# Apply step of the second LayerNorm on GpSimd for three chunks, tail out-projection in one piece, planner constants set anew

## The chip, the cores and the metric

The kernel runs on one core of a Trainium2 chip. Its time is the device time of one execution in microseconds, and the median of several executions is what counts. The core has five engines that each work through their own instruction list in order: TensorE (PE in the profile, its weight loads PEld), VectorE (DVE), ScalarE (ACT), GpSimd (POOL) and SyncE (SP), which here only issues DMAs. Instructions of different engines are ordered by semaphores alone.

## The reference, cut to what matters

The input `x` has 2048 tokens of 640 features. A small product of `c` gives six modulation vectors; then attention with 32 heads of 20 features and a gated bilinear block follow, each behind a LayerNorm without weights.

```python
mod = (silu(c) @ w_mod).reshape(1, 6, 1, 640)
sa, ca, ga, sb, cb, gb = (mod[:, i] for i in range(6))
h = layernorm(x) * (1 + ca) + sa          # first LayerNorm
q, k, v = split(h @ wqkv)                 # 32 heads of 20
p = softmax(q @ k.T * 20 ** -0.5)         # 2048 x 2048 for each head
x = x + ga * ((p @ v) @ wo)               # out-projection
h = layernorm(x) * (1 + cb) + sb          # second LayerNorm
x = x + gb * (((h @ w_gate) * (h @ w_up)) @ w_down)
```

`layernorm(x)` is `(x - mean) / sqrt(var + 1e-5)`. The last step of it, the apply step, takes mean and reciprocal deviation as given and computes `(x - mean) * rs` for each token.

## The kernel before, in words

**Stages.** The queries are cut into five chunks (`CHUNKS`, L431): three of 512 tokens (0 to 2) and two of 256 (3 and 4). Heads are taken four at a time, so a chunk has eight items, 40 in all. For an item PE computes scores against all 2048 keys (L1403), in PSUM banks; a score block is then exponentiated and PE multiplies it with V into bank 7 (L1957). An item ends with a transpose on DVE (L1587), a reciprocal of the softmax sums (L1590), a multiplication on POOL (L1592), a second DVE transpose into `OcT` (L1599) and DMAs on SP's queue that put the rows in place in `Ocp` (L1611).

**Two ways to the exponential.** Most score blocks go to ACT: one Exp over two banks (128x1024), from group 580 on (`HEADG`) over two and three banks in turn (L1439). The others, 99 quads of four blocks (`QUADS` says how many for each item), go to DVE, which builds the exponential from integer operations: an evacuation of each block (L1463), two bit operations (L1495, L1503) and a product (L1500). A block on DVE costs PE two products with V, not one.

**The suffix of a chunk** (function `suffix`) is what follows attention: the out-projection in rounds of 320 columns (L866, in the last chunk L862), its residual sum on DVE (L1682), the second LayerNorm by tiles of 128 tokens, the transposes (L1715) with their evacuation into `h2T` (L1720), the gate and up products with `hprod` (L1815, L1784), and the down product with its residual sum (L1838) and the store. The suffix of chunk 0 runs beside the attention of chunk 1, and so on. Only that of chunk 4, the tail, has no attention beside it. What is left of chunk 3's suffix when attention ends is done there too.

**The second LayerNorm of a tile** is: two statistics instructions (L1696), their aggregation (L1698), epsilon added on POOL (L1699; in the tail on DVE), the power -0.5 on POOL (L1701), and the apply step on DVE (L1703) into `xn2`. The transposes of a chunk outside the tail wait for all of its tiles: four for chunks 0 to 2, two for chunks 3 and 4. The profile leaves digits off names, so `xn2` of chunks 0 to 2 reads `xn`, `mv2` reads `mv`, `rs2` reads `rs`.

**The tail's out-projection.** With `OP_EARLY = 1` each of its four rounds is in two pieces: five matmuls on `Ocp` (rows of the items that are done) may go ahead, and a sixth on `OcT` of the last item is a task of its own that waits for the second transpose (L1599).

**What sets the order.** The kernel's Python holds a planner (class `Sched`): each instruction is a `Task` with an engine, an estimated duration, dependencies and a priority, and a simulated clock picks for each engine the ready task of least priority number. The order found is written out as five fixed instruction lists with semaphore waits. Constants shape it: `GATE_F` spreads the rounds of a chunk's suffix over the next chunk's Exp groups; `HT_L`, `V_L`, `K_LEAD`, `KD_LEAD`, `LATE_A` and `LATE_L` say how far ahead of their item projections are due; `D_LEAD` and `D_RES` place the DVE blocks; `PVMIN`, `PVMAX` and `PVCAP` size batches of products with V; `STEAL_GAP` limits when ACT takes over evacuations from DVE, which it may do in the first 66 us of the plan. Tasks marked `lk` use what DVE and POOL share: the planner never lets one of DVE and one of POOL with that mark overlap. With `lk` 2 a POOL task also yields to any ready DVE task with the mark, and gets a dependency on the last such DVE task.

Of the kernel before, what the change touches and what calls it, by code (L numbers as in the profile page):

```python
# [6 lines left out]
ALU = mybir.AluOpType  # L7
# [18 lines left out]
DMA_SLOW = 0.0015  # L26
DMA_LAT = 1700.0
STEAL_END = 66197.894
STEAL_GAP = 184.697
HAM_W = 3413.3  # L30
HAM_MIN = 2550.0

# [288 lines left out]
def emit_program(nc, sched, nsem_dma=56):  # L321
# [83 lines left out]
    with nc.Block() as block:  # L405
# [20 lines left out]
        def _(e):  # L426
# [4 lines left out]
CHUNKS = ((0, 512), (512, 512), (1024, 512), (1536, 256), (1792, 256))  # L431
QUADS = ((0, 4, 3, 3, 4, 3, 4, 3),
# [4 lines left out]
D_LEAD = 0.383  # L437
NB0, NSS = 2, 3
HEADG = 580
OP_EARLY = 1  # L440
EV_OP = 0.5
T_SPLIT = 1
GU_OUTER = 4
# [1 line left out]
LN2T = 0.6  # L445
# [4 lines left out]
XBACK = 1  # L450
HOLD = 110
PVTOL = 253
XDPRIO = 2.163
TPRIO = 0.75
TAHEAD = 1
GU_ONE = 1
# [3 lines left out]
NPS = 4  # L460
TS_4X, TT_2X = 600.0, 1145.0
WM_GATE = 9
WM_NEED = 1.814
K_DIRECT = (0, 1, 2, 3)
Q_DIRECT = 2
K_LEAD = 0.705
K_ALL = (0,)
KD_LEAD = 0.216
DMA_WINDOW = 900000
D_LATE = 16  # L470
D_RES = 58
PVMIN, PVMAX, PVCAP = 4, 14, 13
PV0 = 0
V_PARTS = [[0, 4], [4, 8]]
V_L1 = 0.2
# [7 lines left out]
PREEMPT = 0.0  # L483
PRE_M = 0.3
PV0N = 1
GATE_F = (0.925, 0.688, 1.105, 0.744, 1.0)
FILL_MIN = 4156.882
FILL_HARD = 0.0
FILL_T0, FILL_TH, FILL_MINH = 2300.0, 17000.0, 7500.0
# [3 lines left out]
LN_POOL = ()  # L493
LN_ACT = [1, 3, 5, 7]
XFIRST = 0
LN2P = 2.447
NALT = 1
OPFIRST = 0
HT_L = 0.105
V_L = 0.225  # L500
LATE_A = 4.5
LATE_L = 2.493
LATEQ = (3,)
LATEQ_A = 2
LATEQ_F = 0.581
QUAD_GAIN = 0.597233983857778
NTERM = 2
XHALF = 1
# [12 lines left out]
def build_kernel(nc, A_x, A_wqkv, A_wo, B_x, B_w_gate, B_w_up, B_w_down, c, w_mod, out):  # L521
# [60 lines left out]
    mhalf = alloc("mhalf", [128, 4], F32)  # L582
# [14 lines left out]
    mv2 = alloc("mv2", [128, NT, 2], F32)  # L597
    sd2 = alloc("sd2", [128, NT], F32)
    rs2 = alloc("rs2", [128, NT], F32)
    invT = alloc("invT", [128, 16], F32)  # L600
# [24 lines left out]
    OT = alloc("OT", [128, 512], F32)  # L625
# [27 lines left out]
    xck = R2.alloc("xck", [128, 4, D], BF16)  # L653
    xn2 = R2.alloc("xn2", [128, 4, D], BF16)
# [57 lines left out]
    def dve(dur, f, deps=(), prio=3.0, **k):  # L712
        return sc.add(Task("dve", dur, f, deps, prio=prio, **k))
# [6 lines left out]
    def pool(dur, f, deps=(), prio=3.0, **k):  # L720
        t = Task("pool", dur, f, deps, prio=prio, **k)
        t.lk = 1
        return sc.add(t)

    def dvl(dur, f, deps=(), prio=3.0, **k):
        t = Task("dve", dur, f, deps, prio=prio, **k)
        t.lk = 1
        return sc.add(t)
# [58 lines left out]
    def load_rest():  # L787
# [5 lines left out]
        for q, f in enumerate((first2[0], first2[1],  # L793
# [12 lines left out]
    p_i0 = pool(150, lambda e: e.memset(ident[:], 0.0), prio=0)  # L806
    p_id = pool(300, lambda e: e.affine_select(ident[:], ident[:], pattern=[[-1, 128]], compare_op=ALU.not_equal,
                                               fill=1.0, base=0, channel_multiplier=1), [p_i0], prio=0)
    p_mh = pool(100, lambda e: e.memset(mhalf[:], -0.5), prio=1)
    p_on = dve(600, lambda e: e.memset(Vf[:, :].rearrange("p (h w) -> p h w", w=VW)[:, :, 0:1], 1.0), prio=-1)  # L810
    d_pz = dve(500, lambda e: e.memset(ps[:, BPV, :], 0.0), [], prio=3.5)
    d_wz = [dve(70, lambda e, w=w: e.memset(w[:, :, D:WKQ], 0.0), prio=0) for w in (wk_sb, wq_sb)]
# [413 lines left out]
    items = [(ci, j) for ci in range(NC) for j in range(NSET)]  # L1226
# [10 lines left out]
    for it, (ci, j) in enumerate(items):  # L1237
        q0, n = CHUNKS[ci]
# [231 lines left out]
    for qi, (it, us) in enumerate(dquads):  # L1470
# [36 lines left out]
        if X_POOL and qi % X_POOL == X_POOL - 1 and qi < len(dquads) - X_LAST and all(  # L1507
# [22 lines left out]
            t = term(fx, [tm, te], TT_2X, "X", src=0, last=True)  # L1530
# [48 lines left out]
    def item_end_tasks(it):  # L1579
        ci, j = items[it]  # L1580
        if ci == NC - 1 and j == 0:
            z_tail[ci] = [pool(1200, lambda e: e.memset(Ocp[:, ci % 2, KD - 1, :], 0.0), list(oc_free[ci - 2]), prio=9)]
        n = CHUNKS[ci][1]
        nb32 = n // 32
        slot = ci % 2
        cell = {}
        t1 = Task("dve", n * 1.1 + 70, lambda e: e.transpose(OT[:, 0:n], ps[:, BPV, 0:n]), [], prio=0.0, name=f"T1.{it}")  # L1587
        t1.acq = [(sOT, "o", 1)]
        item_info[it]["t1"] = t1
        t2 = dve(155, lambda e: e.reciprocal(invT[:, 0:nb32].unsqueeze(2),  # L1590
                                            OT[:, 0:n].rearrange("p (b c) -> p b c", c=32)[:, :, 0:1]), [t1], prio=1.5)
        f3 = lambda e: e.tensor_tensor(  # L1592
            OTn[:, 0:n].rearrange("p (b c) -> p b c", c=32), OT[:, 0:n].rearrange("p (b c) -> p b c", c=32),
            invT[:, 0:nb32].unsqueeze(2).to_broadcast([128, nb32, 32]), ALU.mult)
        if T3_POOL and it < len(items) - 1:
            t3 = pool(n * 2.2 + 200, f3, [t2], prio=0)
        else:
            t3 = dvl(sb_cost(n, 1.04), f3, [t2], prio=1.5)
        t4 = dve(n * 1.1 + 65, lambda e: e.transpose(OcT[:, cell["s"], 0:n], OTn[:, 0:n]), [t3], prio=1.5)  # L1599
        direct = j == NSET - 1 and ci == NC - 1  # L1600
        pcs = [] if direct else oc_pieces(j)
        t4.acq = [(sOcT, "s", max(1, len(pcs)))]

        def on4(task):
            cell["s"] = task.slots["s"]
            sOT.done(0, task)
# [27 lines left out]
    def suffix(ci):  # L1634
# [28 lines left out]
        t_xn2 = []  # L1663
        x1_done = []
        op_last = []
        for tl in range(ntl):
            ev = []
            for hf in range(2):
                mms = []
                for k in range(KD):  # L1670
                    f = qf(320, lambda k=k, tl=tl: Ocp[:, slot, k, tl * 128:(tl + 1) * 128],
                                 lambda k=k, hf=hf: wo_sb[:, k, 320 * hf:320 * hf + 320], k == 0, k == KD - 1 and not tail)
                    mms.append((C320, f))
                fx = qf(320, lambda tl=tl: OcT[:, oc_last[ci]["s"], tl * 128:(tl + 1) * 128],
                              lambda hf=hf: wo7[:, 320 * hf:320 * hf + 320], False, True)
                if tail and not OP_EARLY:
                    mms.append((C320, fx))

                pq = pr(True)

                def after(r, tl=tl, hf=hf, fx=fx, pq=pq):
                    f = lambda e: e.tensor_tensor(xck[:, tl, 320 * hf:320 * hf + 320], ps[:, r.b["b"], 0:320],  # L1682
                                                  xck[:, tl, 320 * hf:320 * hf + 320], ALU.add)
                    if tail and OP_EARLY:
                        fs_ = fx if isinstance(fx, list) else [fx]
                        r.last = sc.add(Task("pe", C320, [lambda e, g_=g_: g_(e, r.b["b"]) for g_ in fs_], [r.last, oc_ready[ci][-1]],
                                             ctr="pex", prio=pq - 1000, name=f"op{ci}.{tl}", mode=r.last.mode))
                    return [dve(ps_cost(320), f, [r.last, d_xc], prio=EV_OP if tail else 1)]
                r = Round(mms, list(oc_ready[ci][:-1] if tail and OP_EARLY else oc_ready[ci]) + t_wo + [d_xc], after, pq, gate=gate(KD * 320),
                          name=f"op{ci}.{tl}")  # L1690
                ev.append(r.evac[0])
                op_last.append(r.last)
            t = t0 + tl
            bn = []
            for hf in range(2):
                bn.append(dve(ps_cost(320), lambda e, tl=tl, hf=hf: e.bn_stats(  # L1696
                    st2[:, tl, 6 * hf:6 * hf + 6], xck[:, tl, 320 * hf:320 * hf + 320]), [ev[hf]], prio=LN2T if tail else LN2P))
            ag = dve(115, lambda e, t=t, tl=tl: e.bn_aggr(mv2[:, t, :], st2[:, tl, :]), bn, prio=LN2T if tail else LN2P)  # L1698
            f1 = lambda e, t=t: e.tensor_scalar(sd2[:, t:t + 1], mv2[:, t, 1:2], EPS, None, op0=ALU.add)  # L1699
            p1 = dve(75, f1, [ag], prio=LN2T if tail else LN2P) if tail else pool(220, f1, [ag], prio=1)  # L1700
            p2 = pool(570, lambda e, t=t: e.tensor_tensor(rs2[:, t:t + 1], sd2[:, t:t + 1], mhalf[:, 0:1], ALU.pow),  # L1701
                      [p1], prio=1)
            t_xn2.append(dvl(360, lambda e, t=t, tl=tl: e.tensor_scalar(  # L1703
                xn2[:, tl, :], xck[:, tl, :], mv2[:, t, 0:1], rs2[:, t:t + 1], op0=ALU.subtract, op1=ALU.mult),
                [p2] + first, prio=LN2T if tail else LN2P))
            x1_done += ev
        oc_free[ci] = op_last[-1:]
        if tail:
# [644 lines left out]
```

## Time and profile before

| what | value |
|---|---|
| median of three executions | 817.66 us (817.46 to 822.7) |
| profiled execution, its own time | 816.77 us |
| its span, first to last instruction | 815.0 us |
| granted TensorE clock | 1.0 throughout |
| ACT busy | 775.9 us, of which Exp (777 instructions) 756.9 us |
| PE busy | 787.8 us |
| DVE busy | 722.7 us |
| POOL busy | 73.3 us |
| first Exp starts, last Exp ends | 16.30 us, 782.43 us |
| apply steps of chunks 0 to 2 on DVE | 12 instructions, 427 ns each on average |
| filler matmuls of PE (L2277), which keep its clock up | 27.3 us |

The profiled execution took 1.8 us more than its span, and the median lies 0.9 us above the profiled execution. "Busy" is the time in which an engine had an instruction in work; instructions of one engine overlap a little, so the mean of one times the count is more than the busy time. Idle time of an engine is put down to the engine whose semaphore came last.

### The profile page before, as it was taken

To read this page: it belongs to the slowest core of one execution; us is meant where nothing else is said; L and a number is where in the kernel's file an instruction comes from. 1 tells how busy PE (TensorE), PEld (TensorE's weight loads), DVE (VectorE), ACT (ScalarE), POOL (GpSimd) and SP (SyncE) were. 2 spreads that over 40 slices of the span, in tenths; PEclk is the share of its full clock that TensorE was granted. 3 is DMA by queue.
4 is the path that set the end of the run, shared out by engine and by line. 5 is a ranking of instruction groups with operands and counts; after the bars stand their busy time and mean duration, and the time that the engine had idled before them with its cause. 6 is when DMAs were issued, how large, how long until landed. Compare 5 with 4: busy or idle time off the path is not lost.

```text
span 815.0 us, 29082 instructions
## 1 busy us (share of the span) xinstructions
PE 787.8 (97%) x12581; PEld 306.3 (38%) x12581; DVE 722.7 (89%) x1272; ACT 775.9 (95%) x821; POOL 73.3 (9%) x105
## 2 busy tenths in 40 slices
PE   9999999999999999999999999999989999999998
PEld 4433333322232332233333223333243344554557
DVE  7989999999989999999999999999998877676663
ACT  6889999999999999999999999999999999999952
POOL 3300000000011000000001000000021000000000
PEclk9999999999999999999999999999999999999999
DMA  9724311113500225100400222002100236116610
GB/s 294 222 84 103 77 39 38 49 49 116 126 19 25 51 66 160 39 5 28 95 6 12 49 53 55 6 20 61 47 8 14 55 86 130 44 31 137 133 37 17
DMA packets 116446, 54.73 MB, mean 67 GB/s; under 512 B 83915, under 2 KB 116319, under 8 KB 116319
## 3 DMA queue, kind: packets, MB, share of 16 engines
q1 hardware_dynamic: 115391, 51.72, 24.8%
q8 instruction: 100, 1.64, 0.9%
q10 hardware_dynamic: 928, 1.15, 0.4%
q14 instruction: 27, 0.22, 0.1%
HBM read 41.85 MB, written 8.41 MB: 62 GB/s over the span
## 4 chain that ended last, share of the span: by engine, by line
ACT 44%; PE 37%; issue 9%; DVE 9%; DMA 1%; ACTq 0%; DVEq 0%
ACT PP L1439 44%; PE ps_all L1403 11%; PE ps_all L866 10%; PE ps_all L1957 7%; DVE DB L1463 3%; PE ps_all L862 3%; PE ps_all L1126 3%; PE ps_all L1062 2%; DVE DSS L1500 1%; DMA wm<-in_w_mod_dram 1%; DVE DSS L1495 1%; DVE DSS L1503 1%; PE ps_all L1023 1%; PE ps_all L887 0%; DVE st L1696 0%
## 5 line engine op out<-in xcount | busy, mean ns | idle before, releaser
L1439 ACT ACTIVATE PP<-ps_all 128x1024 bf16<-128x1024 f32 (+1 forms) x777 | 756.9, 1202 | 5.4 <-PE ps_all L1403 3.9
L1403 PE MATMUL ps_all<-QT,KT 32*128 32x512 bf16 (+1 forms) x2560 | 309.0, 340 | 17.4 <-ACT PP L1439 13.5
L1463 DVE TENSOR_SCALAR DB<-ps_all 128x512 int16<-128x512 f32 x396 | 263.1, 682 | 35.4 <-PE ps_all L1403 34.2
L1403 PEld LDWEIGHTS ps_all<-QT,KT 32*128 32x128 bf16 x2560 | 81.5, 91 | 262.3 <-ACT PP L1439 232.4
L1957 PE MATMUL ps_all<-PP,Vf 128*32 128x512 bf16 (+2 forms) x2092 | 164.3, 342 | 0.1
L1500 DVE TENSOR_TENSOR DSS<-DB,DSS 128x2048 bf16<-128x2048 bf16 x99 | 122.0, 1232 | 0.0
L866 PE MATMUL ps_all<-h2T,stg 128*32 128x512 bf16 (+1 forms) x1808 | 116.7, 338 | 1.6 <-DVE DB L1463 1.1
L1592 POOL TENSOR_TENSOR OTn<-OT,invT 128x512 bf16<-128x512 f32 (+1 forms) x39 | 43.1, 1104 | 604.8 <-DVE invT L1590 604.8
L1957 PEld LDWEIGHTS ps_all<-PP,Vf 128*32 128x32 bf16 (+1 forms) x2092 | 47.2, 94 | 85.2 <-issue 78.5
L1957 PE MATMUL ps_all<-DSS,Vf 128*32 128x512 bf16 (+3 forms) x936 | 77.4, 350 | 0.2
L1495 DVE TENSOR_SCALAR DSS<-DB 128x2048 int16<-128x2048 int16 x99 | 68.2, 689 | 0.8
L1503 DVE TENSOR_SCALAR DSS<-DB 128x2048 int16<-128x2048 int16 x99 | 68.1, 688 | 0.9 <-PE ps_all L1957 0.9
L866 PE MATMUL ps_all<-wd,hprod 128*32 128x320 bf16 (+1 forms) x1364 | 57.9, 280 | 0.1
L866 PEld LDWEIGHTS ps_all<-h2T,stg 128*32 128x32 bf16 x1808 | 40.3, 95 | 36.9 <-issue 17.1
L866 PEld LDWEIGHTS ps_all<-wd,hprod 128*32 128x32 bf16 x1364 | 30.7, 96 | 18.4 <-issue 10.4
L866 PE MATMUL ps_all<-wV,hT 128*32 128x320 bf16 (+1 forms) x704 | 31.6, 289 | 0.1
L1957 PEld LDWEIGHTS ps_all<-DSS,Vf 128*32 128x32 bf16 (+1 forms) x936 | 23.4, 95 | 21.9 <-issue 9.1
L1126 PE MATMUL ps_all<-hT,wq 128*32 128x512 bf16 x375 | 31.1, 382 | 0.2
L1815 DVE TENSOR_TENSOR hprod<-ps_all,gsb 128x512 bf16<-128x512 f32 x36 | 24.6, 684 | 6.0 <-PE ps_all L866 6.0
L866 PE MATMUL ps_all<-wo,Ocp 128*32 128x320 bf16 (+1 forms) x620 | 28.8, 288 | 0.4 <-DVE DB L1463 0.2
L1587 DVE STREAM_TRANSPOSE OT<-ps_all 128x512 f32<-128x512 f32 (+1 forms) x40 | 24.2, 604 | 4.3 <-PE ps_all L1957 4.2
L2277 PE MATMUL ps_all<-ident 128*32 128x512 bf16 x308 | 27.3, 383 | 0.3 <-DVE DB L1463 0.2
(122 smaller groups left out, 516.8 us busy)
## 6 DMA issues: line engine op xcount, KB each, us to landing
stg<-in_B_w_gate_dram SPq DMA_DIRECT2D x50, 160.0 KB
stg<-in_B_w_up_dram SPq DMA_DIRECT2D x50, 160.0 KB
QT<-q_rows SPq DMA_DIRECT2D x22, 128.0 KB
KT<-k_rows SPq DMA_DIRECT2D x84, 32.0 KB
wm<-in_w_mod_dram SPq DMA_DIRECT2D x3, 800.0 KB
x<-in_A_x_dram SPq DMA_DIRECT2D x7, 320.0 KB
xck<-in_A_x_dram SPq DMA_DIRECT2D x3, 640.0 KB
wd<-in_B_w_down_dram SPq DMA_DIRECT2D x1, 1920.0 KB
```

The source lines that it names most:

```text
L866: return lambda e, b: e.matmul(ps[32 * x:32 * x + 32, b, c0 + o:c0 + o + w], lhs()[:, 32 * x:32 * x + 32], rhs() if w == n else rhs()[:, o ...
L1126: f = [lambda e, b_, k=k, x=x: e.matmul(ps[x:x + min(32, w - x), b_, :], wx[:, k, r0 + x:r0 + min(x + 32, w)], hT[tc][:, k, :], tile_posit ...
L1403: ems.append(lambda e, i=i, kt=kt: e.matmul(dstf()[:, i * u.n:(i + 1) * u.n], KT[32 * u.s:32 * u.s + 32, u.j, kt * 128:(kt + 1) * 128], QT ...
L1439: return e.activation(PPs[g % 2][:, cellp["p"], 0:nu * 512], ps[:, b0:b0 + nu, :].rearrange("p b c -> p (b c)"), AFT.Exp, scale=ESCALE)
L1463: return e.tensor_scalar(DB0[:, st_["slot"], x * 512:(x + 1) * 512], bank(cell["b"]), EBIAS, 0.0, op0=ALU.add, op1=ALU.max)
L1495: return e.tensor_scalar(DSS[:, st_["ss"][0], :], DB0[:, st_["slot"], :], 0x7F, 0x3F00, op0=ALU.bitwise_and, op1=ALU.bitwise_or)
L1500: return e.tensor_tensor(d, DB0[:, st_["slot"], :].bitcast(BF16), d, ALU.mult)
L1503: return e.tensor_scalar(DSS[:, st_["ss"][1], :], DB0[:, st_["slot"], :], 0x7F80, 2, op0=ALU.bitwise_and, op1=ALU.bitwise_or)
L1592: f3 = lambda e: e.tensor_tensor(OTn[:, 0:n].rearrange("p (b c) -> p b c", c=32), OT[:, 0:n].rearrange("p (b c) -> p b c", c=32), invT[:, ...
L1815: f = lambda e: e.tensor_tensor(hprod[:, fc, 0:n], ps[:, r.b["b"], 0:n], gsb[:, gs, 0:n], ALU.mult)
L1957: ems.append(lambda e, i=i, kt=kt, stt=stt, stp=stp: e.matmul(ps[32 * s:32 * s + mc, BPV, 0:u.n], Vf[:, (kt * H + 4 * u.j + s) * VW:(kt * ...
L2277: task.emits = [lambda e, x=x: e.matmul(ps[32 * x:32 * x + 32, b_, :].rearrange("p (a b) -> p a b", a=4), ident[:, 32 * x:32 * x + 32], id ...
```

## The change

Three things change. First, the apply step of the second LayerNorm of chunks 0 to 2 becomes a POOL task with an estimate of 760 ns, priority 1 and `lk` 2; chunks 3 and 4 keep it on DVE. Second, `OP_EARLY` is 0: each round of the tail's out-projection has all six matmuls and waits for the second transpose of the last item. Third, constants of the planner have new values, among them `QUADS`: chunk 2 has one DVE quad less, and chunk 4 one more. A second switch, `RC_POOL`, which would move the reciprocal to POOL, is in the code and off; for it one column pair of a small constant tile is set to -1 by another POOL memset.

```diff
-STEAL_GAP = 184.697
+STEAL_GAP = 187.231
...
-         (3, 3, 4, 4, 3, 4, 4, 4),
+         (3, 3, 4, 3, 3, 4, 4, 4),
          (1, 2, 1, 2, 1, 1, 1, 2),
-         (1, 1, 1, 1, 0, 1, 1, 1))
-D_LEAD = 0.383
+         (1, 1, 1, 1, 1, 1, 1, 1))
+D_LEAD = 0.381
...
-HEADG = 580
-OP_EARLY = 1
+HEADG = 579
+OP_EARLY = 0
...
-XDPRIO = 2.163
+XDPRIO = 3.0
...
-WM_NEED = 1.814
+WM_NEED = 1.838
...
-K_LEAD = 0.705
+K_LEAD = 0.755
...
-KD_LEAD = 0.216
+KD_LEAD = 0.212
...
-D_RES = 58
-PVMIN, PVMAX, PVCAP = 4, 14, 13
+D_RES = 63
+PVMIN, PVMAX, PVCAP = 2, 10, 12
...
-GATE_F = (0.925, 0.688, 1.105, 0.744, 1.0)
+XN2_LK = 2
+XN2_POOL = 3
+RC_POOL = 0
+RC_COST = 900
+GATE_F = (0.793, 0.688, 1.105, 0.744, 1.0)
...
-LN2P = 2.447
+LN2P = 2.344
...
-HT_L = 0.105
-V_L = 0.225
-LATE_A = 4.5
-LATE_L = 2.493
+HT_L = 0.02
+V_L = 0.246
+LATE_A = 3.254
+LATE_L = 1.2
...
-LATEQ_F = 0.581
+LATEQ_F = 0.578
...
-    p_mh = pool(100, lambda e: e.memset(mhalf[:], -0.5), prio=1)
+    p_mh = pool(100, lambda e: e.memset(mhalf[:, 0:2], -0.5), prio=1)
+    p_m1 = pool(100, lambda e: e.memset(mhalf[:, 2:4], -1.0), prio=2)
...
-            t_xn2.append(dvl(360, lambda e, t=t, tl=tl: e.tensor_scalar(
-                xn2[:, tl, :], xck[:, tl, :], mv2[:, t, 0:1], rs2[:, t:t + 1], op0=ALU.subtract, op1=ALU.mult),
-                [p2] + first, prio=LN2T if tail else LN2P))
+            fx2 = lambda e, t=t, tl=tl: e.tensor_scalar(
+                xn2[:, tl, :], xck[:, tl, :], mv2[:, t, 0:1], rs2[:, t:t + 1], op0=ALU.subtract, op1=ALU.mult)
+            if XN2_POOL and ci < XN2_POOL:
+                tx = pool(760, fx2, [p2] + first, prio=1)
+                tx.lk = XN2_LK
+            else:
+                tx = dvl(360, fx2, [p2] + first, prio=LN2T if tail else LN2P)
+            t_xn2.append(tx)
```

More of the change, by code (lines that the diff above doesn't have):

```diff
@@ L1589, in item_end_tasks @@
         item_info[it]["t1"] = t1
-        t2 = dve(155, lambda e: e.reciprocal(invT[:, 0:nb32].unsqueeze(2),
-                                            OT[:, 0:n].rearrange("p (b c) -> p b c", c=32)[:, :, 0:1]), [t1], prio=1.5)
+        den = OT[:, 0:n].rearrange("p (b c) -> p b c", c=32)[:, :, 0:1]
+        if RC_POOL and it < len(items) - 1:
+            t2 = pool(RC_COST, lambda e: e.tensor_tensor(invT[:, 0:nb32].unsqueeze(2), den, mhalf[:, 2:3].unsqueeze(2).to_broadcast([128, nb32, 1]), ALU.pow), [t1, p_m1], prio=0)
+        else:
+            t2 = dve(155, lambda e: e.reciprocal(invT[:, 0:nb32].unsqueeze(2), den), [t1], prio=1.5)
         f3 = lambda e: e.tensor_tensor(
@@ L1702, in suffix @@
                       [p1], prio=1)
-            t_xn2.append(dvl(360, lambda e, t=t, tl=tl: e.tensor_scalar(
-                xn2[:, tl, :], xck[:, tl, :], mv2[:, t, 0:1], rs2[:, t:t + 1], op0=ALU.subtract, op1=ALU.mult),
-                [p2] + first, prio=LN2T if tail else LN2P))
+            fx2 = lambda e, t=t, tl=tl: e.tensor_scalar(
[3 more added lines that the diff above has]
+                tx.lk = XN2_LK
+            else:
+                tx = dvl(360, fx2, [p2] + first, prio=LN2T if tail else LN2P)
+            t_xn2.append(tx)
             x1_done += ev
```

## The prediction

> **What bounds the kernel now.** I read the page's busy times and 40 slices first, to see which engine is full and where; then busy times by stage, to see whether that engine ever runs dry; then its waits, to see what it lacks there; then the rows of the operations that are moved.
>
> ```profile
> ## 1 busy us (share of the span) xinstructions
> PE 787.8 (97%) x12581; PEld 306.3 (38%) x12581; DVE 722.7 (89%) x1272; ACT 775.9 (95%) x821; POOL 73.3 (9%) x105
> ...
> ACT   6889999999999999999999999999999999999952
> ```
>
> ACT is full in every slice but the first three and the last two. The view by stage (busy time and count of each engine between two times) says how full, to hundredths:
>
> ```profile
> 16.00:84.00 68.00, 67.45 (x1059) 28.00 (x1051) 61.27 (x125) 61.76 (x71) 11.37 (x23) 1.00 0.50 143
> 84.00:236.00 152.00, 148.36 (x1990) 44.98 (x1986) 144.18 (x229) 151.56 (x166) 9.87 (x6) 1.00 0.25 68
> 236.00:272.00 36.00, 34.87 (x458) 11.29 (x450) 35.97 (x68) 35.98 (x41) 7.51 (x10) 1.00 0.08 23
> ...
> 418.00:438.00 20.00, 18.62 (x291) 6.69 (x283) 19.75 (x40) 20.00 (x23) 4.18 (x9) 1.00 0.03 6
> ...
> 600.00:622.00 22.00, 19.67 (x410) 8.88 (x410) 21.83 (x48) 22.00 (x21) 5.96 (x11) 1.00 0.03 7
> ...
> 740.00:782.00 42.00, 39.83 (x1010) 23.34 (x1010) 26.45 (x55) 42.00 (x38) 1.84 (x3) 1.00 0.49 109
> 782.00:793.00 11.00, 10.73 (x193) 6.70 (x192) 9.02 (x27) 2.39 (x6) 1.28 (x2) 1.00 0.05 16
> 793.00:815.00 22.00, 19.31 (x177) 16.43 (x175) 7.23 (x17) 4.46 (x12) 0.00 (x0) 1.00 0.07 24
> ```
>
> The columns are PE, PEld, DVE, ACT, POOL, then clock, DMA share, GB/s. Three things are to be seen. From 84 us to the last Exp ACT lacks nothing: 35.98 of 36, 20.00 of 20 and 22.00 of 22 us in the three stages where the moved apply steps lie, although DVE is full there too. Between 16 and 84 us ACT lacks 68.00 - 61.76 = 6.24 us. And after the last Exp (782.43 us) PE is the full engine: 10.73 of 11 us until 793, then the gate, up and down products of the tail.
>
> ```profile
> ACT PP L1439 <- PE ps_all L1403: 3.9, 6, 1.3
> ACT PP L1439 <- PE ps_all L1957: 1.1, 1, 1.1
> ACT QT L1083 <- PE ps_all L1062: 0.7, 1, 0.7
> ACT KT L1076 <- PE ps_all L1062: 0.4, 1, 0.4
> ACT Vf L1216 <- PE ps_all L866: 0.3, 1, 0.3
> ```
>
> These are ACT's waits between 20 and 780 us (total, times, longest): 6.4 us, all for PE, nothing for DVE or POOL. So the time is 16.3 us before the first Exp, 766.1 us of Exps, of which some 6 us are waits early on, 32.6 us of tail, and 1.8 us around the span: 816.77 us. DVE is not a term of it. The median is 0.9 us higher; I make the sum against 816.77 and add 0.9.
>
> **The change part by part.** *Apply steps leave DVE.*
>
> ```profile
> L1703 DVE TENSOR_SCALAR xn<-xck,mv,rs 128x640 bf16<-128x640 bf16 x12 | 5.1, 427 | 0.1
> ```
>
> 12 instructions of 427 ns free 5.1 us of DVE, 1.7 us in each stage. The number of Exps stays (99 quads before and after), so ACT's work stays, and ACT already has 77.98 of 78 us in these stages. Value 0; at best 0.5 us if Exps that start some ns late hide a little.
>
> *They arrive on POOL.* No row shows this operation there. The nearest:
>
> ```profile
> L1592 POOL TENSOR_TENSOR OTn<-OT,invT 128x512 bf16<-128x512 f32 x24 | 33.4, 1392 | 459.9 <-DVE invT L1590 459.9
> ...
> L1299 POOL COPY SCb<-scol 128x640 bf16<-128x640 bf16 x1 | 0.7, 716 | 3.1 <-ACT hT L1029 3.1
> ```
>
> The COPY has the same size and type and one input: 0.716 us. The two-input product takes 1.05 us at its median, by elements 1.05 x 640 / 512 = 1.31 us. I take 0.75, next to the COPY, because the apply step has one tensor input; the ends are 0.72 and 1.31. 12 x 0.75 = 9 us on an engine that is 9% busy. Behind it in POOL's queue wait the next tile's epsilon and power steps (0.22 and 0.57 us) and now and then a product L1592. That product's buffer is wanted again by the next item, some 22 us later (the first transposes of items lie at 218.6, 242.4 and 267.0 us), so a delay of 1 or 2 us is covered; without that cover DVE would wait, as it does for 1.8 us in all today. The transposes that need the four tiles get their last one 0.75 - 0.43 = 0.3 us later, plus what the step waits for DVE (its mark makes it yield to DVE and adds a semaphore wait on the last marked DVE task): up to 1.2 us, the length of one product L1500. PE has filler to do in these stages (27.3 us in all, 288 of 308 matmuls between 208 and 267, 397 and 442, 578 and 626 us), so being late costs filler. Value 0; if a transpose blocks the scores behind it in PE's list, at most 3 x 1.2 = 3.6 us.
>
> *Sharing between DVE and POOL.* At 244.36 us a POOL product starts, and the DVE product that starts inside it is stretched:
>
> ```profile
> 244.48 2.07 DVE L1500 TENSOR_TENSOR DSS<-DB,DSS 128x2048 bf16<-128x2048 bf16 x1
> ```
>
> Its median is 1.22 us, so one collision costs DVE 0.85 us. ACT had 35.98 of 36 us around it: the price did not reach the end. The planner keeps marked tasks apart and the new ones also wait for DVE's semaphore, so I expect one to three collisions more, at 0 for the path. The bounds come with the first rival.
>
> The Trainium skill speaks against this part. "SBUF - State Buffer", section "Who interferes with whom", says that VectorE and GpSimd share a port pair as an exclusive lock, and that the later one stands still for the whole instruction; the 2.07 us row agrees. "GPSIMD Engine Reference", section "Engine selection", sends elementwise work to VectorE. By the first rule taken at its worst each new step would stop one DVE instruction, and by the second nothing would be gained; the row of ACT's 35.98 us says that neither reaches the end while ACT has scores in store.
>
> *The tail's out-projection in one piece.* Before, 20 of 24 matmuls went ahead and four followed the last transpose at 784.76 us; the last ended at 786.11. Now all 24 follow. Thirteen of them took 1.94 us, 0.149 each, so 24 end at 784.76 + 3.58 = 788.34 us, 2.2 us later. The last tile's chain from there: sum 0.48, statistics 0.44, aggregation 0.20, epsilon 0.15, power 0.55 to 0.73, makes 790.2 to 790.3, with four engine hops about 790.7 us. In the profile that apply step started at 790.74, because DVE did four sums in a row (1.68 us), statistics, and sums of chunk 3 between. PE fills the space before 784.76 with chunk 3's down products, of which 148 matmuls (37 x 0.142 = 5.3 us) lie behind the last Exp. Value 0, bounds -0.5 and +2.2.
>
> *One DVE quad from chunk 2 to chunk 4.* Four blocks more go to ACT in chunk 2, four fewer in chunk 4. From 740 to 782 us 38 Exps of 2.5 blocks took 42.00 us, 0.442 a block, so attention of chunk 4 is 4 x 0.442 = 1.8 us shorter and chunk 2's as much longer. But chunk 3's suffix has to fit beside chunk 4, where PE has 2.2 us to spare in 42; what does not fit is added to the 5.3 us behind the last Exp, where PE is full. Between 0 and +1.8 us; I take the middle, +0.9.
>
> *Constants.* What matters is the head, where PE is full (67.45 of 68) with projections. `LATE_L` 2.49 to 1.2 holds back projections that are due more than 1.2 items later, where 2.49 was allowed, and leaves PE to the scores that ACT waits for; `HT_L` and `V_L` move the transposes and V the same way or against it. Between -6.2 us (all early waits go) and +2 (two more like the longest, 1.3 and 1.1, less what they replace); I take a third of the waits, -2.1. `GATE_F` for chunk 0 brings its suffix forward in a stretch with 10.1 us of filler: 0. `HEADG` by one hands a bank over one group earlier: 0. The batches of products with V (`PVMIN` and so on) change in size, not in number: 0. No DMA is added. SP's loads of gate and up weights are reordered beside them; ACT and PE show no wait for a DMA after 20 us. The added memset (0.10 us) lies in 4.7 us of POOL idle: 0.
>
> Sum: 816.77 + 0.9 - 2.1 = 815.6; at the level of the median 816.5 us.
>
> **The rivals.** *Slower: collisions.* Every new POOL step stops a DVE product: 12 x 0.85 = 10.2 us, less the 5.1 freed. DVE is full in these stages (35.97 of 36), so it passes on once score banks run out: 817.7 + 5.1 = 822.8. It decides from six collisions on. For it: five DVE instructions are stretched so today beside 39 POOL products. Against it: ACT did not notice them.
>
> *Slower: the tail.* All 2.2 us of the later out-projection and all 1.8 us of chunk 3's rest show: 817.7 + 4.0 = 821.7. For it: PE is full from 782 to 793. Against it: the two overlap, since the rest fills the wait.
>
> *Faster: the head.* All early waits go: 817.7 - 6.2 = 811.5. For it: all are PE's. Against it: PE's projections have to be done anyway.
>
> *No effect:* the plan differs and no term moves: 817.7, inside the forecast's own range.
>
> **How the numbers follow.** Forecast with no effect 0.60, own range 814.5 (head -4.1) to 819 (tail +1.8, head 0); tail 0.13; collisions 0.12; head 0.10; other 0.05. The range goes from 812.5, between forecast and head, to 821.7, the tail's price, and leaves out the collisions and half of the head. Three executions of the kernel before span 0.6%, so about 1% is what can be told from no change. Faster by that means under 809.5: more than all early waits, 0.03. Slower means over 825.8: collisions and tail together, 0.05. Within: 0.92.
>
> **What would show it.** The apply row on POOL at 0.72 to 0.80 us, x12; L1500's longest at 2.07 us still, in few cases; ACT full in the three stages; its early waits under 6.2 us; the tail's first gate matmul within 32.6 - 22.5 = 10.1 us of the last Exp, give or take 1.8. I am wrong if ACT waits for PE or DVE in the three stages, if the apply step takes over 1.3 us, or if the tail grows by over 2 us.

## The result, and the profile after

| | before | after |
|---|---|---|
| median (6 executions each) | 817.56 us | 848.66 us |
| lowest, highest | 816.67, 822.7 | 843.74, 850.7 |
| profiled execution, its span | 816.77, 815.0 us | 848.4, 846.8 us |
| mean granted TensorE clock in it | 1.000 | 0.972 |
| first Exp starts, last Exp ends | 16.30, 782.43 us | 16.22, 813.38 us |
| last Exp to the end of the span | 32.6 us | 33.4 us |

The change makes the kernel slower: 1.0367 times the time, 95% interval 1.0345 to 1.0388, which is 31 us. The forecast was 816.5 us with no visible effect. Nearly all of the 31 us lie between the first and the last Exp (797.2 against 766.1 us); the tail has 0.8 us of them.

From the page of the kernel after: busy times, ACT's, POOL's and the clock's slices, and two groups of instructions.

```profile
PE 804.5 (95%) x12557; PEld 310.2 (37%) x12557; DVE 725.9 (86%) x1260; ACT 779.2 (92%) x821; POOL 106.8 (13%) x118
...
ACT  7889999999887699999999699999998999999952
POOL 3300000010015000000005300000034000001000
PEclk9999999999989599999999799999997999999999
...
L1444 ACT ACTIVATE PP<-ps_all 128x1024 bf16<-128x1024 f32 (+1 forms) x777 | 760.2, 1178 | 33.5 <-PE ps_all L1408 31.4
...
L1711 POOL TENSOR_SCALAR xn<-xck,mv,rs 128x640 bf16<-128x640 bf16 x12 | 32.2, 2689 | 12.0 <-DVE DSS L1505 11.5
```

The last line is the surprise: the apply step takes 2.69 us on POOL on average, not 0.75, and not 1.31, my upper end. Its shortest, median and longest, in nanoseconds:

```profile
L1711 POOL TENSOR_SCALAR xn<-xck,mv,rs x12: 2497/2516/4184, 265.8 to 642.2; 128x640 bf16<-128x640 bf16 x12
```

The other lines show where that comes out. ACT's work is nearly unchanged (Exps 760.2 against 756.9 us), but it now stands idle for PE. In three places ACT and the clock have dents where POOL has peaks; a dent of ACT and the clock just before the first of them (220 to 240 us) has no such peak.

PE's longest waits in the kernel after, and under them nothing that matters:

```profile
PE ps_all L1728 <- POOL xn L1711: 12.2, 3, 6.8
PE ps_all L1408 <- ACT PP L1444: 12.1, 47, 0.6
PE ps_all L871 <- DMA Ocp<-OcT: 3.9, 1, 3.9
```

The second is the old pacing of the scores by ACT (13.5 us before). The first and the third are new: the transposes of the second LayerNorm wait for POOL once in each of chunks 0 to 2 (6.8, 4.8 and 0.6 us), and the out-projection of chunk 0 waits for a DMA. ACT passes both on:

```profile
ACT PP L1444 <- PE ps_all L1408: 31.4, 31, 6.8
```

The busy times by stage show them (columns PE, PEld, DVE, ACT, POOL, clock, DMA share, GB/s):

```profile
220.00:240.00 20.00, 15.72 (x183) 4.44 (x181) 12.27 (x19) 14.38 (x16) 0.77 (x1) 0.83 0.41 101
240.00:266.00 26.00, 24.62 (x350) 7.97 (x348) 25.64 (x49) 26.00 (x30) 5.71 (x10) 1.00 0.07 20
266.00:276.00 10.00, 3.54 (x42) 0.96 (x42) 4.47 (x7) 4.60 (x6) 10.00 (x4) 0.81 0.09 27
276.00:293.00 17.00, 16.59 (x122) 4.46 (x122) 9.61 (x16) 10.78 (x11) 1.31 (x2) 0.51 0.06 14
...
465.00:484.00 19.00, 14.11 (x132) 4.69 (x132) 13.00 (x21) 12.35 (x14) 8.12 (x4) 0.73 0.01 2
640.00:662.00 22.00, 19.70 (x304) 7.80 (x298) 16.33 (x30) 18.63 (x16) 5.70 (x7) 0.77 0.06 13
```

The first, third and fourth of these stretches in the kernel before:

```profile
220.00:240.00 20.00, 18.98 (x273) 6.19 (x271) 17.41 (x30) 20.00 (x23) 2.28 (x3) 1.00 0.17 37
...
266.00:276.00 10.00, 9.94 (x131) 3.00 (x129) 10.00 (x18) 10.00 (x12) 1.37 (x1) 1.00 0.19 48
276.00:293.00 17.00, 16.91 (x241) 5.26 (x242) 16.78 (x27) 17.00 (x20) 1.90 (x1) 1.00 0.28 66
```

Read ACT's column. Before, it was full in these three stretches; now it lacks 5.6, 5.4 and 6.2 us. In the third stretch POOL is the only engine that is full. In the fourth, PE is full by its busy time (16.59 of 17 us) but does 122 matmuls where it did 241 before, at a clock of 0.51. Three lines in order of time show how the stage begins and ends:

```profile
265.84 10.42 POOL L1711 TENSOR_SCALAR xn<-xck,mv,rs 128x640 bf16<-128x640 bf16 x4 [6.54 <-DVE DSS L1505]
...
276.41 0.37 PE L1728 MATMUL ps_all<-ident,xn 128*128 128x128 bf16 x2 [6.79 <-POOL xn L1711]
...
277.36 1.02 ACT L1444 ACTIVATE PP<-ps_all 128x1024 bf16<-128x1024 f32 x1 [6.76 <-PE ps_all L1408]
```

Four apply steps run back to back for 10.42 us. PE's list, fixed for steps of 760 ns, has the transposes where four such steps would have ended, 4 x (2.6 - 0.76) = 7.4 us sooner; PE stands at the first of them for 6.79 us. Behind it in the list are the scores, and ACT stands for 6.76 us as well. In chunk 1 the four steps take longer still:

```profile
460.40 11.67 POOL L1711 TENSOR_SCALAR xn<-xck,mv,rs 128x640 bf16<-128x640 bf16 x4 [5.00 <-DVE DSS L1505]
```

### The profile page after: what moved, and what is told of

The parts are those of the page before. It is cut to its first block, busy times and chain, and to the rows that moved or that the text cites. A ratio compares the mean times of both kernels' runs of the same rounds, so it can differ in the third digit from the quotient of the medians.

```text
span 846.8 us, 29000 instructions
## 1 busy us (share of the span) xinstructions
PE 804.5 (95%) x12557; PEld 310.2 (37%) x12557; DVE 725.9 (86%) x1260; ACT 779.2 (92%) x821; POOL 106.8 (13%) x118
## 4 chain that ended last, share of the span: by engine, by line
ACT 37%; PE 33%; DVE 15%; issue 8%; POOL 5%; DMA 1%; SPq 0%; ACTq 0%; DVEq 0%; POOLq 0%
ACT PP L1444 37%; PE ps_all L1408 10%; PE ps_all L871 9%; PE ps_all L1970 7%; DVE DB L1468 6%; POOL xn L1711 4%; PE ps_all L867 3%; DVE DSS L1505 2%; DVE DSS L1508 2%; DVE DSS L1500 1%; PE ps_all L1131 1%; PE ps_all L1067 1%; PE ps_all L1728 1%; DMA wm<-in_w_mod_dram 1%; DVE OT L1592 1%
## 5 line engine op out<-in xcount | busy, mean ns | idle before, releaser
L1444 ACT ACTIVATE PP<-ps_all 128x1024 bf16<-128x1024 f32 (+1 forms) x777 | 760.2, 1178 | 33.5 <-PE ps_all L1408 31.4
L1408 PE MATMUL ps_all<-QT,KT 32*128 32x512 bf16 (+1 forms) x2560 | 314.6, 346 | 16.1 <-ACT PP L1444 12.1
L1970 PE MATMUL ps_all<-PP,Vf 128*32 128x512 bf16 (+2 forms) x2088 | 167.9, 349 | 0.3 <-DVE OT L1592 0.2
L871 PE MATMUL ps_all<-h2T,stg 128*32 128x512 bf16 (+1 forms) x1780 | 119.8, 347 | 1.1 <-DVE DB L1468 0.4
L1500 DVE TENSOR_SCALAR DSS<-DB 128x2048 int16<-128x2048 int16 x99 | 72.2, 730 | 1.0
L1508 DVE TENSOR_SCALAR DSS<-DB 128x2048 int16<-128x2048 int16 x99 | 69.3, 700 | 0.0
L1592 DVE STREAM_TRANSPOSE OT<-ps_all 128x512 f32<-128x512 f32 (+1 forms) x40 | 24.1, 603 | 13.6 <-PE ps_all L1970 13.5
L1711 POOL TENSOR_SCALAR xn<-xck,mv,rs 128x640 bf16<-128x640 bf16 x12 | 32.2, 2689 | 12.0 <-DVE DSS L1505 11.5
L2290 PE MATMUL ps_all<-ident 128*32 128x512 bf16 x352 | 30.9, 386 | 0.4
```

Of the source, the lines that this page charges most:

```text
L871: return lambda e, b: e.matmul(ps[32 * x:32 * x + 32, b, c0 + o:c0 + o + w], lhs()[:, 32 * x:32 * x + 32], rhs() if w == n else rhs()[:, o ...
L1408: ems.append(lambda e, i=i, kt=kt: e.matmul(dstf()[:, i * u.n:(i + 1) * u.n], KT[32 * u.s:32 * u.s + 32, u.j, kt * 128:(kt + 1) * 128], QT ...
L1444: return e.activation(PPs[g % 2][:, cellp["p"], 0:nu * 512], ps[:, b0:b0 + nu, :].rearrange("p b c -> p (b c)"), AFT.Exp, scale=ESCALE)
L1500: return e.tensor_scalar(DSS[:, st_["ss"][0], :], DB0[:, st_["slot"], :], 0x7F, 0x3F00, op0=ALU.bitwise_and, op1=ALU.bitwise_or)
L1508: return e.tensor_scalar(DSS[:, st_["ss"][1], :], DB0[:, st_["slot"], :], 0x7F80, 2, op0=ALU.bitwise_and, op1=ALU.bitwise_or)
L1711: fx2 = lambda e, t=t, tl=tl: e.tensor_scalar(xn2[:, tl, :], xck[:, tl, :], mv2[:, t, 0:1], rs2[:, t:t + 1], op0=ALU.subtract, op1=ALU.mult)
```

## The experiments

The theory after the result was **A**: the apply step's true price on POOL, against the 760 ns with which the order was made, holds up PE at the transposes, and PE's standing brings the half clock. Rivals: **C**, that POOL's work as such costs (collisions, DVE held up); **D**, that the constants and the tail cost; **E**, that the yielding of `lk` 2 costs.

### 1. What the step costs by itself

A small kernel with none of the computation of the reference: each form three times on POOL.

> A small kernel that leaves the whole computation out: it loads 512 rows of x and runs, three times each on an otherwise idle core, nine operations of 128x640 on POOL, then the apply step on DVE. Theory A (the step is dear on POOL in itself): two per-partition scalars, 16 bit in and out, takes 2.50 us here too, as it did in the changed kernel beside an idle DVE (2497 ns at 273.77 us). What makes it dear is open: if it is the two scalars read from memory, immediates bring it to about 0.75 us and one scalar to between; if it is the two operations, one operation halves it, scalar or immediate; if it is the number of elements, 320 columns take half. Theory C (it is dear because DVE holds what both share): 0.7 to 0.8 us here. A copy should be 0.72 us, a product of two tensors 1.3 us, DVE 0.43 us.

From the groups of instructions of this kernel:

```profile
L62 POOL TENSOR_SCALAR r_base<-xin,col 128x640 bf16<-128x640 bf16 x3 | 7.5, 2499 | 5.0 <-DVE x L50 5.0
...
L64 POOL TENSOR_SCALAR r_imm<-xin 128x640 bf16<-128x640 bf16 x3 | 7.0, 2348 | 0.0
L66 POOL TENSOR_SCALAR r_one<-xin,col 128x640 bf16<-128x640 bf16 x3 | 5.6, 1882 | 0.0
...
L72 POOL TENSOR_SCALAR r_half<-xin,col 128x320 bf16<-128x320 bf16 x3 | 4.3, 1432 | 0.0
L78 POOL TENSOR_TENSOR r_tt<-xin 128x640 bf16<-128x640 bf16 x3 | 4.1, 1390 | 0.0
...
L70 POOL COPY r_copy<-xin 128x640 bf16<-128x640 bf16 x3 | 2.0, 719 | 0.0
```

Mean nanoseconds stand after the bar's comma. The step is 2.50 us with nothing beside it, so this price does not come from DVE's work beside it: 2.499 - 1.432 = 1.067 us for 320 elements, 3.33 ns an element and 0.37 us fixed. Immediate numbers in place of the two pointers save 0.15 us, one operation in place of two 0.62 us; f32 input or output changes nothing (2499 both). On DVE the same form takes 445 ns in this kernel. What the copy shows of POOL does not carry over to this form: with one operation and no pointer (1807 ns) it still costs more than a product of two tensors.

### 2. The step alone, on the plan before

```diff
+XN2_LK = 2
+XN2_POOL = 3
...
+            if XN2_POOL and ci < XN2_POOL:
+                tx = pool(760, fx2, [p2] + first, prio=1)
+                tx.lk = XN2_LK
```

> The kernel before with the apply steps of chunks 0 to 2 on POOL (estimate 760 ns, the same yielding to DVE), all constants and the two-piece out-projection as before. Theory A: 817.6 + 25 = 843, between 835 and 850, with PE waiting some us before the transposes in each stage. Theory B: under 822.

850.16 us, 1.0407 (1.0344 to 1.0471). PE's waits:

```profile
PE ps_all L1722 <- POOL xn L1705: 8.4, 3, 6.2
```

The step alone, with the old constants and the old tail, costs as much as the whole change, at the upper end of what was expected. Constants and tail are not needed for the loss. It is divided otherwise, though: PE stands less for POOL (8.4 against 12.2 us), the mean clock is 0.970 (0.972), and 37.9 us lie behind the last Exp (33.4).

### 3. The same lists, a cheap instruction in the step's place

The five lists of the kernel after stay as they are; only the apply step is a copy of the same size, its computation left out.

```diff
-                tx = pool(760, fx2, [p2] + first, prio=1)
+                tx = pool(760, lambda e, tl=tl: e.tensor_copy(xn2[:, tl, :], xck[:, tl, :]), [p2] + first, prio=1)
```

> The changed kernel, its plan and its instruction lists unaltered, but the twelve POOL steps are copies of xck into xn2 (the apply step of the second LayerNorm is left out for chunks 0 to 2). A copy of this shape took 0.72 us, the plan has 0.76 for the step, so the plan's price is now true. Theory A (price of 2.50 us against a plan of 0.76, by which PE stands before the transposes): PE's waits for xn, 12.2 us, go; the half clock at 272, 470 and 648 us goes; the loss of 25 us in the three stages goes and the time is 820 to 828, with the wait for Ocp at 228.6 us still there. Theory C (collisions and yielding between DVE and POOL, or late transposes through the yielding alone): over 838. Theory B (the constants): over 840.

825.41 us, 1.0093 (1.0072 to 1.0113). Its busy times by stage:

```profile
220.00:240.00 20.00, 15.72 (x191) 4.60 (x195) 12.65 (x19) 14.76 (x17) 0.91 (x1) 0.83 0.40 101
...
266.00:276.00 10.00, 9.78 (x117) 3.41 (x115) 9.05 (x18) 10.00 (x12) 3.30 (x5) 1.00 0.10 28
276.00:293.00 17.00, 16.85 (x232) 5.12 (x232) 16.96 (x26) 17.00 (x20) 0.00 (x0) 1.00 0.19 45
```

With the price that the plan was made for, ACT is full again in the stage (10.00 and 17.00), PE no longer waits for POOL, and 23 of the 31 us are gone. As order and semaphore waits are the same, the length of the step makes these 23 us, not the order, the constants or the yielding. A shorter step also lies less beside DVE's work, so C is left to experiment 6. What is left, 8 us, has its dent between 220 and 240 us, as in the kernel after (ACT 14.76 of 20).

### 4. A price between

The same edit with a product of the tile with itself (a two-tensor form) in place of the copy; the apply step is left out here too.

> The changed kernel, plan and lists unaltered, with a product of xck with itself in place of the apply step on POOL in chunks 0 to 2 (the apply step is left out). It took 1.39 us alone, between the copy (0.72) and the step (2.50). Theory A: four steps are 4 x 0.63 = 2.5 us longer than planned, so PE stands up to 2.5 us in chunk 0, less in chunk 1, not in chunk 2; time 826 to 832, against 825.4 with the copy and 848.7 with the step. Rival (a price that does not matter until PE is made to stand): as the copy, under 826. Rival C, where collisions count: a third of the way, 832 or more.

831.77 us, 1.0153 (1.0118 to 1.0189), as expected. The profiled execution was a short one of 825.79 us, with PE's waits for POOL of at most 1.2 us; the others lay at 831.7 to 831.9 with a mean clock of 0.988 to 0.990 against its 0.998. So even a step of 1.25 us, inside the ends of the prediction, costs some 6 us more than the copy in three of four executions, and the clock is lower in these. Only the short one left a profile, so where the others lose is not shown.

### 5. What of the loss is the clock

Nothing of the computation changes. While PE would stand before the first transpose of chunks 0 to 2, it does 24, 18 and 6 idle products.

```diff
+    for ci, n_ in ((0, 24), (1, 18), (2, 6)):
+        i = next(i for i, t in enumerate(sc.order["pe"]) if t.name == f"h2T{ci}.0")
...
+        w_ = Task("pe", 216.0 * n_, [f] * n_, [d for d in t.deps if d.eng != "pool"], ctr="pex", name="warm")
+        sc.order["pe"].insert(i, w_)
```

> The changed kernel with 24, 18 and 6 filler matmuls of 0.216 us put into PE's list ahead of the first transpose of chunks 0, 1 and 2, where PE stood 6.8, 4.8 and 0.6 us. Nothing else is moved. Theory (part of the loss is the half clock that follows standing): the half clock at 272 and 470 us goes, PE still stands, and of 25 us lost the 12.2 of standing stay: 848.7 falls by 6 to 12 us, to 837 to 843. Rival (the half clock costs nothing, as PE has room): within 2 us of 848.7.

837.31 us, 1.0239 (1.0221 to 1.0256). Its busy times by stage:

```profile
266.00:276.00 10.00, 8.59 (x66) 3.13 (x65) 3.98 (x6) 4.12 (x5) 9.77 (x4) 1.00 0.09 27
276.00:293.00 17.00, 17.00 (x183) 5.33 (x181) 13.75 (x22) 14.52 (x16) 1.05 (x1) 0.80 0.11 26
```

ACT still lacks 5.9 us in the first of them, since the transposes come no sooner, but in the second only 2.5 where it lacked 6.2: of the 17 us only 6.8 are at half clock. The mean clock of the execution rises from 0.972 to 0.992. So at least 848.7 - 837.3 = 11.4 us of the loss are what PE's standing does to the clock afterwards; the other 837.3 - 825.4 = 11.9 us are the step's price itself, with what these 6.8 us of half clock cost.

### 6. The right price in the planner

```diff
-                tx = pool(760, fx2, [p2] + first, prio=1)
+                tx = pool(2600, fx2, [p2] + first, prio=1)
```

> The changed kernel with one number altered: the planner takes 2600 ns for the apply step on POOL, not 760. The work on POOL is the same. Theory A (not the work but its wrong place in the order): PE's longest wait before the transposes falls from 6.8 to under 1.5 us, the clock stays at 1.0 in these stages, and the time is 822 to 830. Theory C (POOL's 30 us of work, or its collisions with DVE, are what costs): 840 or more, however the order is planned. Theory B: about 848.

844.57 us, 1.0325 (1.0288 to 1.0361): a miss for A. The dents in the stages are nearly gone (first to last Exp 777.2 us, no wait of PE for POOL), but the tail after the last Exp is 48.7 us, with 358 gate and up products of chunk 3. POOL's order in time shows why:

```profile
265.44 5.02 POOL L1711 TENSOR_SCALAR xn<-xck,mv,rs 128x640 bf16<-128x640 bf16 x2 [6.54 <-DVE DSS L1505]
...
278.09 2.50 POOL L1711 TENSOR_SCALAR xn<-xck,mv,rs 128x640 bf16<-128x640 bf16 x1 [3.52 <-DVE DSS L1505]
285.24 2.50 POOL L1711 TENSOR_SCALAR xn<-xck,mv,rs 128x640 bf16<-128x640 bf16 x1 [4.66 <-DVE DSS L1505]
```

The four steps of a chunk are spread over 22 us, and wait for a DVE product again and again. That could be C or E, so the mark was changed:

```diff
-XN2_LK = 2
+XN2_LK = 1
```

> The changed kernel with the planner's price for the apply step at 2600 ns, as in the run with the true price, and with mark 1 in place of 2: the step no longer yields to DVE nor waits for its last marked task. Theory E (with the true price the loss sits in the yielding: steps of 2.5 us find no room between DVE's marked tasks, the transposes come at 291, 479 and 665 us, and chunk 3's products fall behind the last Exp): transposes of chunk 0 start before 283 us, the tail is under 40 us and the time 824 to 836. Rival C (30 us of work on POOL, or its collisions with DVE, cost by themselves): 842 or more.

830.47 us, 1.0158 (1.0134 to 1.0182), with the price still at 2600. The group of the step in this kernel:

```profile
L1711 POOL TENSOR_SCALAR xn<-xck,mv,rs 128x640 bf16<-128x640 bf16 x12 | 32.8, 2730 | 1.0
```

POOL works as long as in the change (32.8 against 32.2 us) and no longer waits for DVE (1.0 against 12.0 us of idle time ahead). A chunk's transposes follow sooner, at 262, 453 and 628 us (291, 479 and 665 with `lk` 2). So C falls and E holds: with the right price it was the yielding, with the plan that it leads to, that cost 14 us, not POOL's work. In the change itself the yielding is no such term, as experiment 3 has it too.

### 7. The constants, without the step

```diff
-XN2_POOL = 3
+XN2_POOL = 0
```

> The changed kernel with the apply steps of all chunks back on DVE, all other constants and the one-piece out-projection kept. Theory A (apply step of 2.5 us on POOL where the plan has 0.76, so that PE stands before the transposes): the losses of ACT in the three stages go, 13.3 + 7.3 + 4.3 = 25 us, and 848.7 falls to about 824; the wait for the DMAs into Ocp at 228.6 us, 6 us of loss, stays, since the plan is the same up to there. Theory B (the new constants do it): 840 or more.

832.73 us, 1.0172 (1.014 to 1.0204), 9 us more than expected: the out-projection's wait stays (4.0 us), and 38.3 us lie behind the last Exp, 5 us more than in the whole change. Taken with experiment 6, the step on POOL, rightly priced and not yielding, is no dearer than the step on DVE under these constants (830.5 against 832.7), though the two plans differ.

### 8. Where the constants cost

Experiment 3's kernel, with two constants of the head set back:

```diff
-LATE_A = 3.254
-LATE_L = 1.2
+LATE_A = 4.5
+LATE_L = 2.493
```

> The copy in place of the apply step on POOL (left out for chunks 0 to 2), as before, and LATE_A and LATE_L back at 4.5 and 2.493. Theory D (these two put q_rows and weight loads ahead of the DMAs into Ocp in SP's list): the wait for Ocp of 3.9 us and the half clock at 231 us go, ACT loses 1 us or less between 220 and 240 us, where it lost 6. Rival: another constant does it, and the wait stays. The whole time may rise all the same, since the suffixes are planned anew.

823.21 us, 1.0073 (1.0056 to 1.009). Its first stretch:

```profile
220.00:240.00 20.00, 18.98 (x279) 6.23 (x271) 17.41 (x29) 20.00 (x24) 2.35 (x3) 1.00 0.13 29
```

The dent is gone, wait and half clock with it, and the Exps end 6 us sooner; 4.6 of these come back behind the last Exp. What had happened in the kernel after is on SP's queue (issues in order of time):

```profile
220.81 1.54 SPq L1177 DMA_DIRECT2D q_rows<-KPA  x2
224.40 0.81 SPq L1199 DMA_DIRECT2D QT<-q_rows  x2
225.25 0.44 SPq L1768 DMA_DIRECT2D stg<-in_B_w_gate_dram  x1
...
226.87 0.78 SPq L1619 DMA_DIRECT2D Ocp<-OcT  x1
227.70 1.23 SPq L1177 DMA_DIRECT2D q_rows<-KPB  x2
228.98 2.29 SPq L1619 DMA_DIRECT2D Ocp<-OcT  x3
```

The later projection puts a write of `q_rows` and the read back of it ahead of the `Ocp` moves. SP stands at the read from 222.35 to 224.40 us until the write has landed, weight loads and a second write follow, and the `Ocp` moves start at 226.87 and 228.98 us, though their input was there at 222.6. Before, theirs was there at 225.62 us, and they went at 225.65 and 227.44.

The other way round, these two constants alone on the kernel before (`LATE_A` 4.5 to 3.254, `LATE_L` 2.493 to 1.2):

> The kernel before with LATE_A 3.254 and LATE_L 1.2 alone, the two constants that delay projections of chunk 0. Theory D (these put writes and reads of q_rows and loads of weights into SP's list ahead of the DMAs into Ocp, so that PE's out-projection waits for them at about 230 us and the clock drops once): PE waits some 3 to 4 us for Ocp, time 822 to 826. Rival, as on record: they relieve the head, ACT's waits before 84 us fall by about 2 us, time 814 to 817.

823.88 us, 1.0082 (1.0055 to 1.0109). The time fits D, the mechanism does not: here the wait for `Ocp` is only 1.1 us, and only 0.8 us of ACT are lost there. ACT loses mostly at 560 and 618 us instead: 1.7 us in a wait for scores and 3.5 us in one for products with V. Its early waits stay as they were. Why this plan loses there stays open.

### 9. The quads and the tail

The new `QUADS` alone on the kernel before:

```diff
-         (3, 3, 4, 4, 3, 4, 4, 4),
+         (3, 3, 4, 3, 3, 4, 4, 4),
...
-         (1, 1, 1, 1, 0, 1, 1, 1))
+         (1, 1, 1, 1, 1, 1, 1, 1))
```

> The kernel before with the DVE quad moved from chunk 2 to chunk 4 and nothing else. On record: 0 to +1.8 us, as chunk 4's attention is 1.8 us shorter and chunk 3's suffix has less room; 817.6 to 819.5, and the tail after the last Exp longer by that. Rival: the whole plan behind item 16 shifts and PE loses more, over 821.

821.48 us, 1.0045 (1.003 to 1.006), by the ratio 3.7 us: first to last Exp is 765.7 us (766.1 before), and the tail is 37.0 us, 4.5 more, with 80 gate and up products of chunk 3 behind the last Exp.

The tail's out-projection in one piece alone (`OP_EARLY` 1 to 0 on the kernel before):

> The kernel before with the tail's out-projection in one piece and nothing else. As on record the last matmul of it ends 2.2 us later and the transposes do not; theory: 817.0 to 818.5. Rival (tail): the full 2.2 us show, 819.8.

818.43 us, 1.0002 (0.9988 to 1.0015): no difference.

## Why the prediction was wrong

The result lies 27 us over the upper end of the range. Of the 31 us, at most 12 are the step's price by itself, at least 11 the half clock behind it, and 8 what the constants cost with lists made for a cheap step, by the differences of experiments 5 and 3 to the change and to the kernel before. These shares hold for the lists of the change: with the old constants the step alone costs 32 us (experiment 2), and planned anew without it the constants cost 15 (experiment 7).

**The step that failed first: "I take 0.75, next to the COPY, because the apply step has one tensor input; the ends are 0.72 and 1.31."** The true price is 2.50 to 2.69 us. The choice went by the number of tensor inputs; the runs show that the form decides. And the upper end, a product scaled by elements, was no bound: it is another form. The product's row itself reads 1392 ns, of which I took the median, 1.05 us; the mean would have made the end 1.74 us, still too low. Epsilon, the same form on one column, stood at 0.22 us, but one element for each partition tells nothing of 640, so that row could not close the range either. Where no row has the operation, the bound upward should have stayed open, and the question should have been at what price the step decides.

**The step behind it: "Value 0; if a transpose blocks the scores behind it in PE's list, at most 3 x 1.2 = 3.6 us."** The place was right: it is just this blocking that happened, in all three stages. The size was wrong three times over. The delay was taken as that of one step and one yield; but four steps of a chunk follow each other on one queue before the transposes, so the error in the price counts four times, 7.4 us for the first chunk. "Being late costs filler" holds only for a delay that the list was made with: the lists are fixed, PE comes to the transpose at its old place, and the filler that could have filled the gap stands elsewhere. And PE's standing was given no price beyond its length.

**The half clock was not in the sum at all.** The trace before shows a clock of 1.00 in every stretch, so no row priced it. But the filler matmuls in that list, 27.3 us "which keep its clock up", were a sign that standing has a price beyond its length; experiment 5 puts it at 11.4 us or more.

**The constants: "-2.1", and "ACT and PE show no wait for a DMA after 20 us" for SP's order.** The head brought 0.7 us (ACT 62.48 busy us between 16 and 84 against 61.76), and 0.8 were lost again until 220 us. The reasoning on SP was of the kind "no wait today"; it did not ask how much slack the `Ocp` moves had. They had little, and the projections that I counted only on PE move two DMAs each on that queue, one waiting for the other.

**The quad: "+0.9", between 0 and 1.8.** The place was right (chunk 3's suffix grows behind the last Exp), the size 3.7 us by itself. In the change as a whole the tail grew by only 0.8 us. That comes with the order of its lists and not with the time lost in the stages: with the copy, on the same lists, the tail is also 33.4 us, while planned anew without POOL's steps it is 38.3. So the effects of the constants, taken one by one, do not add up.

**Right were:** DVE's relief is worth nothing (the trace shows no ACT wait for it); the out-projection in one piece is worth nothing.

**Collisions** were put at one to three more, at 0 for the path; this was half right. Against five before, twelve of DVE's products and bit operations take over 1.2 times their median: two products (the longest again 2.07 us) and ten bit operations, for some 4 us more in all. Seven more is above the six from which the first rival was to decide. But experiment 6, with 14 of them and the same work on POOL, is no slower than the step on DVE. What did reach PE is the stretching of POOL's own steps: one took 2.93 us in chunk 0 and one 4.18 us in chunk 1, each beside a stretched bit operation of DVE, and as four steps lie ahead of one wait, the 0.4 and 1.7 us over 2.50 lengthen PE's stands. No run tells what that is worth at the end; it is a small part of the 12.2 us of standing. So the first rival had the right sign by a mechanism that explains little of the loss.

Of the three signs that I gave for being wrong, two came: ACT waited for PE in the stages, and the step took over 1.3 us.

**What stays open:** why the two late constants cost at 560 and 618 us on the plan before, how the 8 us of the constants divide among those not tried alone (`GATE_F`, `PVMIN`, `D_RES` and others), and why the plans of experiments 2, 6 and 7 leave a longer tail than that of the change. No kernel here beats the one before.

## What to carry to other kernels

Price an operation that moves to another engine by the same form on that engine, or leave the upper end open and work out from which price it decides: here half a microsecond over the planner's 760 ns already cost (experiment 4), because four steps add up ahead of one wait. In a kernel with fixed lists, an underestimate can cost more than the work itself, as the waiting engine has its other work behind the wait. Count what a stand does afterwards (here as much again in half clock), and count, for each moved piece, the DMAs that it pushes ahead of others on a shared queue.

## What the runs showed of the hardware

**The clock after a stand.** The busy times of the kernel after in short stretches:

```profile
266.00:272.20 6.20, 3.54 (x42) 0.96 (x42) 4.47 (x7) 4.60 (x6) 6.20 (x3) 1.00 0.01 4
268.77:272.18 3.41, 0.84 (x10) 0.20 (x6) 2.65 (x4) 1.83 (x2) 3.41 (x2) 1.00 0.02 7
272.30:276.00 3.70, 0.00 (x0) 0.00 (x0) 0.00 (x0) 0.00 (x0) 3.70 (x2) 0.50 0.21 64
...
282.00:288.00 6.00, 6.00 (x50) 1.26 (x48) 4.50 (x8) 3.83 (x5) 0.00 (x0) 0.50 0.01 3
288.00:292.60 4.60, 4.60 (x39) 0.88 (x35) 1.83 (x4) 2.91 (x4) 0.00 (x0) 0.50 0.11 28
292.80:296.00 3.20, 3.20 (x51) 0.86 (x39) 3.08 (x6) 3.07 (x4) 0.00 (x0) 1.00 0.31 69
...
644.24:647.65 3.41, 2.00 (x32) 1.06 (x32) 2.34 (x5) 3.06 (x4) 1.03 (x2) 1.00 0.01 3
```

The clock halves while PE stands, and stays at half until 292.7 us, 16 us after PE has begun again, although PE is busy by its modelled ends (6.00 of 6, 4.60 of 4.60). In all, 47.8 us of this execution are at half clock, in four pieces of 6.8, 20.5, 10.2 and 10.2 us. The first three come within stands of 3.9 (for `Ocp`), 6.8 and 4.8 us. The last comes without a long one: in the 3.41 us ahead of it PE was busy for 2.00 us, with waits of 0.6 us for POOL and 0.8 us for DVE. The Trainium skill ("TensorE: Matmul & The Clock Gate", Part 1) puts the gate's window at about 3.4 us, halves the clock after at least one idle one and restores it after at least one busy one. The pieces here are multiples of that window. That one busy window is enough to bring the clock back is not what the 20.5 us show, nor did the gate wait for a window without any work: ahead of the second piece PE was busy for 0.84 of 3.41 us, ahead of the last for 2.00.

**The spread of the kernel before** goes with it: of 27 executions beside the experiments, the 20 with a mean clock of 1.0 took 816.9 to 818.8 us. The other seven had 0.994 to 0.998; five of them took 819.1 to 822.7 us, two 817.9 and 818.4.

**POOL's forms.** For 128x640 bf16, a copy takes 0.72, a product of two tensors 1.39, and a two-operation tensor-scalar 2.50 us, against 0.44 us on DVE for the last. Rows of one form say little of another on this engine.
